# Scores of the first two pairs of heads from 64-row halves instead of stacked copies, in a fused attention and two-mixer kernel

## The chip, the cores and the metric

One core of one Trainium2 chip runs the whole program in one launch. The metric is the device time of that launch in microseconds, lower is better. Engines are named as in the profile: PE is TensorE (PEld its weight loads), DVE is VectorE, ACT is ScalarE, POOL is GpSimd, SP is the queue that issues most DMAs.

## The reference

The inputs q, k, v have 4 batches, 12 heads, 448 positions and 64 numbers a head. Everything is float32 outside; two mixers follow the attention.

```python
def _attn_ref(q, k, v, g_q, g_k):
    q_n, k_n = rmsnorm(q, g_q), rmsnorm(k, g_k)      # x / sqrt(mean(x*x) + 1e-6) * g
    scores = q_n @ k_n.T / sqrt(64)
    attn = exp(scores - max(scores))
    return (attn / (attn.sum(-1) + 1e-9)) @ v

def _moe_ref(x, U, V, w_ch1, w_ch2):
    u = x + ((x.T @ U) @ V).T
    return u + relu(u @ w_ch1) @ w_ch2               # w_ch1: 768 x 3072

def _moe2_ref(x, w_tok1, w_tok2, w_ch1, w_ch2):
    u = x + (relu(x.T @ w_tok1) @ w_tok2).T
    return u + relu(u @ w_ch1) @ w_ch2               # w_ch1: 768 x 1536
```

## The kernel before, in words

A matmul runs on a rounded float32 type, so each operand that must be exact is split into a high half (a rounded copy, on ACT) and a low half (the rest, on DVE or POOL), and a product is the sum of high by high, low by high and high by low.

Attention works on pairs of heads: 24 pairs, 48 heads. The generator `attention` (line 513) steps t from -8 over all heads. In a step t it issues the scores and probabilities of the head two ahead (`softmax`, line 450), interleaved with the weighting of the values by head t (`weigh`, line 471). Then it prepares later pairs: `turn_pair` and `split_v` for the pair of head t+3, `fetch_heads` (loads of q and k) for t+7, `load_pair` for t+5. The first 24 heads run alone; the others run beside the first mixer, advanced by the loop `run` at a fixed ratio.

`load_pair` (line 369) squares q and k (line 378; on DVE for pairs 0, 2 and 3, on POOL for the others), sums the squares on DVE (line 379), forms the reciprocal root with ACT's Ln and Exp and a Newton step (lines 381 to 389), and multiplies q and k by it (line 397), which gives qn and kn. The square tile `sq` has one buffer.

`turn_pair` (line 412) transposes qn and kn of both heads on PE into `tt` (line 418), so that rows 0 to 63 hold the first head and rows 64 to 127 the second. ACT writes the high half and DVE the low half into a tile `both` (lines 425 and 426 for q, 429 and 430 for k). `both` has one buffer for q and one for k. Since the scores need each head on all 128 rows, SP copies the halves by DMA into stacked tiles: `qs` holds a head's q, high on rows 0 to 63 and low below; `ks` holds k's high (first half) and low (second half), each twice (lines 440 to 446). Pair 0 takes 12 such copies (its ks in four pieces), each later pair 8.

`softmax` (line 450) then needs two products per chunk of 112 positions. The score tile `sc` comes from a PSUM pool of three banks. DVE takes the negated maximum (line 459), ACT the exponential with its sum (line 461), POOL and DVE the reciprocal and the scaling of two chunks at a time (lines 464 to 468).

`weigh` transposes the probabilities into `pt` (line 487), copies them (ACT and DVE) and multiplies them by the values into `pv`. `split_v` (line 403) splits the values of every second head (ACT line 149, POOL line 150).

The framework orders the instructions of each engine before the run, with its own model of time, by the order of the program and the dependences; `tc.issue_after(ins)`, used by the helper `behind(name)` (line 83), adds an edge: what the block issues on that instruction's engine stands behind it. `marks` holds the instructions by name. Each engine and the SP queue then run in that fixed order.

Of the kernel before, what the change touches and what calls it, by code (L numbers as in the profile page):

```python
# [24 lines left out]
def attention_then_two_mixers(  # L25
# [343 lines left out]
    def load_pair(b, hp, turn, qk):  # L369
# [5 lines left out]
        for i, t in enumerate((qr, kr)):  # L375
            sq = pools["at"].tile([CP, 2 * NC4, D], F32, tag="sq", bufs=AT["sq"], name="sq")
            tt = t.rearrange("p h c d -> p (h c) d")
            mul(sq, tt, tt)
            nc.vector.reduce_sum(ms[:, i], sq, axis=AX.X)
# [15 lines left out]
        for i, (nm, t, n) in enumerate((("qn", qr, qn), ("kn", kr, kn))):  # L395
            n.append(pools["at"].tile([CP, NC4, 2, D], F32, tag=nm, bufs=AT["qn"], name=nm))
            mul(
                n[0].rearrange("p c h d -> p h c d"), t, scale(i, [CP, 2, NC4, D]))
        qn, kn = qn[0], kn[0]
# [12 lines left out]
    def turn_pair(qn, kn, first=False, second=False):  # L412

        parts = []
        for n, scale in ((qn, gg), (kn, None)):
# [12 lines left out]
            else:  # L428
                nc.scalar.activation(hi, tt, AF.Copy)
                nc.vector.tensor_sub(lo, tt, f(hi))  # L430
# [3 lines left out]
        for j in range(2):  # L434
            rows = slice(j * D, (j + 1) * D)
            qs = pools["at"].tile([P, S], F32R, tag="qs", bufs=3, name="qs")
            ks = pools["at"].tile([P, 2, S], F32R, tag="ks", bufs=3, name="ks")
            for u in range(2):
                half = slice(u * D, (u + 1) * D)
                if not first:  # L440
                    nc.sync.dma_start(f(ks[half]), f(kk[rows]))
                nc.sync.dma_start(f(qs[half]), f(qq[rows, u]))
            if first:
                for i in range(2):
                    for u in range(2):
                        nc.sync.dma_start(f(ks[u * D:(u + 1) * D, i]), f(kk[rows, i]))
            res.append((qs, ks[:, 0], ks[:, 1]))
        return res

    def softmax(pr, qs, ks, kt):  # L450
        for c in range(NC4):
            if c % 2 == 0:
                sm = pools["at"].tile([CP, 2], F32, tag="sm", bufs=6, name="sm")
            sc = psum("s", [CP, S], "sc")
            cs = slice(c * CP, (c + 1) * CP)
            mm(sc, qs[:, cs], ks, True, False)
            mm(sc, qs[:, cs], kt, False, True)
            nm = pools["at"].tile([CP, 1], F32, tag="nm", bufs=8, name="nm")
            nc.vector.tensor_reduce(nm, sc, axis=AX.X, op=ALU.max, negate=True)  # L459
            p = pools["pp"].tile([CP, S], F32, tag="p", bufs=AT["p"], name="p")  # L460
            nc.scalar.activation(p, sc, AF.Exp, bias=nm, accum_out=sm[:, c % 2:c % 2 + 1])  # L461
            pr.append(p)
            if c % 2:
                nc.gpsimd.tensor_scalar_add(sm, sm, 1e-9)
                nc.vector.reciprocal(sm, sm)  # L465
                for i in range(2):
                    x = pr[c - 1 + i]
                    nc.gpsimd.tensor_scalar(x, x, sm[:, i:i + 1], 1.0, op0=ALU.mult, op1=ALU.mult)  # L468
# [44 lines left out]
    def attention(pairs, seam):  # L513
# [7 lines left out]
        def soft(h):  # L521
            if not 0 <= h < n:
                return iter(())
            probs[h] = []
            return softmax(probs[h], *turned[h // 2][h % 2])

        for t in range(-8, n):
# [4 lines left out]
            steps = [soft(t + ahead) if t >= seam or t + ahead < seam else iter(())]  # L532
# [17 lines left out]
            if 0 < h < n:  # L550
                turned[h // 2] = turn_pair(*loaded[h // 2][:2], second=h == 2)
                values[h // 2] = split_v(loaded[h // 2][2], pairs[h // 2][2])
# [4 lines left out]
            if 0 <= h < n:  # L557
                loaded[h // 2] = load_pair(
                    *pairs[h // 2][:2], h // 2, fetched.pop(h // 2))
                if h == 0:  # L560
                    turned[0] = turn_pair(*loaded[0][:2], first=True)
                    values[0] = split_v(loaded[0][2], pairs[0][2])
# [626 lines left out]
```

## Time and profile before

| | |
|---|---|
| median of 3 runs | 1529.53 us (1521.19 to 1531.46) |
| the profiled execution's own time | 1526.91 us |
| its span, first to last instruction | 1525.1 us |
| PE busy | 1436.3 us (94%) |
| DVE, POOL, ACT busy | 1170.3, 902.3, 745.6 us |
| mean granted clock of PE | 0.985 |

The durations come from the one profiled execution. A busy share is a mean over stages with different limits. In a timeline row the columns are the start in us from the span's start, the time that the merged group took, the engine (SPq is SP's queue of DMA issues), the line, the operation, out<-in, sizes, how many instructions are merged, and in brackets the idle time of the engine before, with what ended it. A matmul's row begins with its start and ends when its result is written, so two that follow closely overlap.

### The profile page before, as it was taken

What the parts mean: (1) busy time and instruction counts of PE and PEld (TensorE: products, weight loads), DVE (VectorE), ACT (ScalarE), POOL (GpSimd) and SP (SyncE); (2) the same over time, 40 slices, a digit from 0 to 9 for tenths busy, and PEclk for the clock granted to TensorE, in tenths of its full rate; (3) what the DMA queues carried; (4) which work ended last, traced back from release to release, by engine and by line L of the source; (5) the groups of instructions that cost most, each with busy time, mean ns of one, the idle gap of its engine ahead of it and who ended that gap; (6) DMA issues with size and microseconds to landing.
All of it is one profiled execution on the core that took longest, in us unless ns stands there. A gap on an engine that the chain in (4) does not pass through costs nothing.

```text
span 1525.1 us, 22086 instructions
## 1 busy us (share of the span) xinstructions
PE 1436.3 (94%) x7396; PEld 1271.5 (83%) x7396; DVE 1170.3 (77%) x1805; ACT 745.6 (49%) x1508; POOL 902.3 (59%) x943
## 2 busy tenths in 40 slices
PE   4899988999999999999999999999999999989997
PEld 3666767888888889888898998888999998979996
DVE  6888877888787788676758675477898988577886
ACT  4687755666566665444535343335343431334421
POOL 5889936777766565455655454047777755213842
PEclk9999979999999999999999999999999999999999
DMA  6676646777766565765637664355445463323343
GB/s 170 151 174 153 151 163 208 245 212 224 236 209 199 166 209 188 247 231 189 221 120 248 227 238 143 102 194 154 157 148 163 147 196 118 120 83 120 126 123 103
DMA packets 144385, 266.06 MB, mean 174 GB/s; under 512 B 12832, under 2 KB 104448, under 8 KB 144160
## 3 DMA queue, kind: packets, MB, share of 16 engines
q1 hardware_dynamic: 143952, 264.65, 55.6%
q8 instruction: 59, 0.97, 0.3%
q14 instruction: 54, 0.44, 0.1%
q10 hardware_dynamic: 320, 0.00, 0.0%
HBM read 149.72 MB, written 79.10 MB: 150 GB/s over the span
## 4 chain that ended last, share of the span: by engine, by line
PE 52%; DVE 8%; DMA 4%; POOL 3%; ACT 2%; issue 2%; SPq 0%; DVEq 0%; POOLq 0%; ACTq 0%
PE ps_x L79 23%; PE ps_p L79 10%; PE ps_g L79 10%; PE ps_t L79 2%; PE ps_u L79 2%; DVE w_bits L136 1%; DVE w_bits L131 1%; DVE w_bits L132 1%; POOL w L150 1%; PE pv L79 1%; ACT w_bits L130 1%; PE pt L487 1%; PE sc L79 1%; POOL w_bits L139 1%; DMA qs<-both 1%
## 5 line engine op out<-in xcount | busy, mean ns | idle before, releaser
L79 PE MATMUL ps_x<-gs,w 128*128 128x448 f32 x1440 | 326.0, 373 | 7.6 <-DVE gs L656 3.9
L79 PE MATMUL ps_g<-u,w 128*128 128x448 f32 x1440 | 312.7, 370 | 4.0 <-DMA w<-h_a 1.6
L79 PEld LDWEIGHTS ps_x<-gs,w 128*128 128x128 f32 x1440 | 267.9, 191 | 34.5 <-DVE gs L656 6.9
L79 PEld LDWEIGHTS ps_g<-u,w 128*128 128x128 f32 x1440 | 270.2, 189 | 27.6 <-DMA w<-h_a 1.8
L79 PE MATMUL ps_x<-gs,w_b 128*128 128x448 f32 x1026 | 226.5, 366 | 6.9 <-DVE xT L852 3.9
L139 POOL TENSOR_TENSOR w_bits<-w_bits,w_round 128x768 uint32<-128x768 uint32 (+3 forms) x80 | 145.1, 1814 | 121.0 <-DVE w_bits L136 68.9
L79 PEld LDWEIGHTS ps_x<-gs,w_b 128*128 128x128 f32 x1026 | 191.9, 188 | 24.4 <-DVE xT L852 5.0
L150 POOL TENSOR_TENSOR w<-w_bits,w 128x768 fp32r<-128x768 f32 (+3 forms) x82 | 148.1, 1816 | 82.9 <-ACT w L149 74.8
L686 DVE TENSOR_TENSOR xT<-ps_x,xT 128x448 f32<-128x448 f32 x216 | 132.2, 618 | 43.5 <-PE ps_x L79 41.2
L150 POOL TENSOR_TENSOR w_b<-w_f,w_b 128x384 fp32r<-128x384 f32 x104 | 119.0, 1157 | 68.2 <-ACT w_b L149 67.9
L468 POOL TENSOR_SCALAR p<-p,sm 112x448 f32<-112x448 f32 x192 | 131.4, 697 | 19.4 <-DVE sm L465 16.1
L79 PE MATMUL sc<-ks,qs 128*112 128x448 f32 x384 | 125.2, 412 | 18.5 <-ACT p L461 15.2
L461 ACT ACTIVATE p<-sc,nm 112x448 f32<-112x448 f32 x192 | 121.5, 635 | 37.8 <-DVE nm L459 36.4
L300 POOL TENSOR_TENSOR w_f<-w_f 128x384 f32<-128x384 f32 x26 | 29.1, 1118 | 176.1 <-DMA w_f<-c_a 99.0
L459 DVE TENSOR_REDUCE nm<-sc 112x1 f32<-112x448 f32 x192 | 116.0, 614 | 12.4 <-PE sc L79 11.9
L487 PEld LDWEIGHTS pt<-ident,p 112*112 112x112 f32 x768 | 88.6, 134 | 32.2 <-issue 9.1
L487 PE MATMUL pt<-ident,p 112*112 112x112 f32 x768 | 109.3, 260 | 3.0 <-DVE pl L502 1.9
L498 ACT ACTIVATE ph<-pt 112x448 fp32r<-112x448 f32 (+1 forms) x168 | 88.3, 545 | 38.4 <-PE pt L487 37.5
L131 DVE TENSOR_SCALAR w_bits<-w_bits 128x768 f32<-128x768 f32 (+3 forms) x80 | 65.2, 815 | 52.4 <-ACT w_bits L130 52.3
L135 ACT ACTIVATE w_round<-w_raw 128x768 uint32<-128x768 uint32 (+3 forms) x80 | 69.9, 874 | 66.4 <-POOL w_bits L139 60.0
L502 DVE TENSOR_TENSOR pl<-pt,ph 112x448 fp32r<-112x448 f32 x144 | 86.9, 615 | 18.3 <-ACT ph L498 17.8
L130 ACT ACTIVATE w_bits<-w_raw 128x768 f32<-128x768 f32 (+3 forms) x80 | 70.0, 875 | 57.5 <-POOL w L150 31.1
(141 smaller groups left out, 2718.0 us busy)
## 6 DMA issues: line engine op xcount, KB each, us to landing
w_raw<-in_moe_w_ch_dram SPq DMA_DIRECT2D x72, 768.0 KB, 5.1
w_b<-h_a SPq DMA_DIRECT2D x65, 384.0 KB, 4.3
h_a<-w SPq DMA_DIRECT2D x56, 384.0 KB, 2.7
ks<-both SPq DMA_DIRECT2D x92, 224.0 KB, 3.7
c_a<-w_bits SPq DMA_DIRECT2D x40, 384.0 KB, 4.4
w_f<-c_a SPq DMA_DIRECT2D x40, 384.0 KB, 3.1
h_b<-w SPq DMA_DIRECT2D x32, 384.0 KB, 2.5
w_b<-h_b SPq DMA_DIRECT2D x29, 384.0 KB, 3.8
```

Source lines behind the costliest of these rows:

```text
L79: nc.tensor.matmul(o, lhsT=l, rhs=r, start=start, stop=stop)
L130: nc.scalar.activation(f(w), f(high), AF.Abs)
L131: nc.vector.tensor_scalar_max(f(w), f(w), TINY)
L139: nc.gpsimd.tensor_tensor(w, w, r, op=ALU.add)
L150: nc.gpsimd.tensor_sub(lo, w, f(hi))
L459: nc.vector.tensor_reduce(nm, sc, axis=AX.X, op=ALU.max, negate=True)
L461: nc.scalar.activation(p, sc, AF.Exp, bias=nm, accum_out=sm[:, c % 2:c % 2 + 1])
L468: nc.gpsimd.tensor_scalar(x, x, sm[:, i:i + 1], 1.0, op0=ALU.mult, op1=ALU.mult)
L487: nc.tensor.transpose(pt[:, c * CP:(c + 1) * CP], pr[c][:, kc * CP:(kc + 1) * CP], ident[:CP, :CP],)
L498: nc.scalar.activation(ph, pt, AF.Copy)
L502: nc.vector.tensor_sub(pl, pt, f(ph))
L686: nc.vector.tensor_add(xT[:, dc], px, xT[:, dc])
```

## The change

For the first two pairs (heads 0 to 3) `turn_pair` is called with `direct=True`: it returns the halves in `both` themselves, on the 64 rows of each head, with three products per chunk (high by high, low by high, high by low), and makes no stacked copies. `softmax` takes several heads, each with its list of products, and issues product i of all heads before product i+1. In step t = -2 it is called for heads 0 and 1 together, so their chunks alternate and their products lie on rows 0 to 63 and 64 to 127; heads 2 and 3 follow one at a time in steps 0 and 1.

New edges: the sums of squares of pair 1 stand behind pair 0's kn on DVE; the squares of pair 2 stand behind the low half of pair 0's k; the value splits of pairs 0 and 1 are issued together in step -2, ACT's part behind the high half of pair 0's k, POOL's part behind pair 1's kn. All other pairs go as before.

```diff
-            mul(sq, tt, tt)
-            nc.vector.reduce_sum(ms[:, i], sq, axis=AX.X)
+            with behind("klo" if turn == 2 else None):
+                mul(sq, tt, tt)
+            with behind("kn" if turn == 1 else None):
+                nc.vector.reduce_sum(ms[:, i], sq, axis=AX.X)
...
-            mul(
+            ins = mul(
                 n[0].rearrange("p c h d -> p h c d"), t, scale(i, [CP, 2, NC4, D]))
+        if turn < 2:
+            marks["kn"] = ins
...
-    def turn_pair(qn, kn, first=False, second=False):
+    def turn_pair(qn, kn, first=False, second=False, direct=False):
...
-                nc.scalar.activation(hi, tt, AF.Copy)
-                nc.vector.tensor_sub(lo, tt, f(hi))
+                khi = nc.scalar.activation(hi, tt, AF.Copy)
+                klo = nc.vector.tensor_sub(lo, tt, f(hi))
+                if first:
+                    marks.update(khi=khi, klo=klo)
...
             rows = slice(j * D, (j + 1) * D)
+            if direct:
+                (qh, ql), (kh, kl) = [[x[rows, i] for i in range(2)] for x in (qq, kk)]
+                res.append([(qh, kh), (ql, kh), (qh, kl)])
+                continue
...
-                if not first:
-                    nc.sync.dma_start(f(ks[half]), f(kk[rows]))
+                nc.sync.dma_start(f(ks[half]), f(kk[rows]))
                 nc.sync.dma_start(f(qs[half]), f(qq[rows, u]))
-            if first:
-                for i in range(2):
-                    for u in range(2):
-                        nc.sync.dma_start(f(ks[u * D:(u + 1) * D, i]), f(kk[rows, i]))
-            res.append((qs, ks[:, 0], ks[:, 1]))
+            res.append([(qs, ks[:, 0]), (qs, ks[:, 1])])
...
-    def softmax(pr, qs, ks, kt):
+    def softmax(*heads):
+        sums = [None] * len(heads)
         for c in range(NC4):
...
+            scs = [psum("s", [CP, S], "sc") for _ in heads]
+            n = len(heads[0][1])
+            for i in range(n):
+                for sc, (_, products) in zip(scs, heads):
+                    l, r = products[i]
+                    mm(sc, l[:, cs], r, i == 0, i == n - 1)
...
+            hs = (0, 1) if t == -2 else (t + ahead,) if t >= 0 else ()
+            steps = [soft(*hs) if t >= seam or t + ahead < seam else iter(())]
...
-                turned[h // 2] = turn_pair(*loaded[h // 2][:2], second=h == 2)
-                values[h // 2] = split_v(loaded[h // 2][2], pairs[h // 2][2])
+                turned[h // 2] = turn_pair(*loaded[h // 2][:2], second=h == 2, direct=h == 2)
+                for i in (0, 1) if h == 2 else (h // 2,):
+                    with behind("khi" if h == 2 else None), behind("kn" if h == 2 else None):
+                        values[i] = split_v(loaded[i][2], pairs[i][2])
...
-                    turned[0] = turn_pair(*loaded[0][:2], first=True)
-                    values[0] = split_v(loaded[0][2], pairs[0][2])
+                    turned[0] = turn_pair(*loaded[0][:2], first=True, direct=True)
```

## Rows read from the trace of the kernel before

**Rows 1.** The page: TensorE's busy time, and its granted clock in 40 slices.

```profile
PE 1436.3 (94%) x7396; PEld 1271.5 (83%) x7396; DVE 1170.3 (77%) x1805; ACT 745.6 (49%) x1508; POOL 902.3 (59%) x943
PEclk9999979999999999999999999999999999999999
```

**Rows 2.** Stretches: length, busy PE, PEld, DVE, ACT, POOL (instructions), clock, DMA share, GB/s.

```profile
25.00:42.20 17.20, 13.68 (x61) 8.96 (x60) 12.79 (x28) 11.24 (x33) 13.08 (x26) 0.90 0.78 188
42.20:190.00 147.80, 135.83 (x782) 100.67 (x781) 128.64 (x264) 112.00 (x303) 131.94 (x244) 0.99 0.64 156
...
432.00:1525.10 1093.10, 1057.39 (x5381) 964.83 (x5379) 819.25 (x1146) 465.56 (x845) 581.61 (x463) 0.99 0.52 169
```

**Rows 3.** Timeline, 8 to 18 us: pair 0 up to its first scores.

```profile
8.52 0.68 DVE L379 TENSOR_REDUCE ms<-sq 112x8 f32<-112x512 f32 x1
...
9.12 0.17 DVE L389 TENSOR_TENSOR rs<-rs,nt 112x16 f32<-112x16 f32 x1
...
9.40 1.19 POOL L150 TENSOR_TENSOR vs<-vr,vs 112x256 fp32r<-112x256 f32 x1 [1.75 <-ACT vs L149]
9.92 1.22 DVE L397 TENSOR_TENSOR kn<-kr,rs 112x512 f32<-112x512 f32 x1
...
12.24 0.54 ACT L429 ACTIVATE both<-tt 128x448 fp32r<-128x448 f32 x1 [0.44 <-PE tt L418]
...
13.40 0.68 DVE L426 SCALAR_TENSOR_TENSOR both<-tt,gg,both 128x448 fp32r<-128x448 f32 x1
...
14.00 0.68 DVE L379 TENSOR_REDUCE ms<-sq 112x8 f32<-112x512 f32 x1
...
14.59 0.61 DVE L430 TENSOR_TENSOR both<-tt,both 128x448 fp32r<-128x448 f32 x1
14.66 2.47 SPq L446 DMA_DIRECT2D ks<-both  x4
...
17.72 1.43 PE L79 MATMUL sc<-ks,qs 128*112 128x448 f32 x3
```

**Rows 4.** Timeline, 22 to 34 us: pair 1, heads 1 and 2.

```profile
22.66 0.54 ACT L429 ACTIVATE both<-tt 128x448 fp32r<-128x448 f32 x1
...
25.05 2.84 SPq L441 DMA_DIRECT2D ks<-both  x4
...
27.15 0.65 PE L79 MATMUL sc<-ks,qs 128*112 128x448 f32 x2
...
29.33 1.04 PE L79 MATMUL sc<-ks,qs 128*112 128x448 f32 x4 [1.53 <-DMA ks<-both]
...
31.85 0.63 ACT L425 ACTIVATE both<-tt,gg 128x448 fp32r<-128x448 f32 x1 [2.39 <-PE pt L487]
...
33.15 1.71 PE L79 MATMUL sc<-ks,qs 128*112 128x448 f32 x4 [1.99 <-ACT p L461]
```

**Rows 5.** Timeline, 36 to 43 us: pair 2, weighting, and head 4's first scores.

```profile
36.87 2.76 SPq L441 DMA_DIRECT2D ks<-both  x4
...
40.43 0.55 PE L487 MATMUL pt<-ident,p 112*112 112x112 f32 x4
...
40.75 0.64 PE L79 MATMUL sc<-ks,qs 128*112 128x448 f32 x2
...
41.22 0.92 PE L79 MATMUL pv<-ph,vr 112*128 112x448 f32 x2
...
42.18 0.57 PE L79 MATMUL sc<-ks,qs 128*112 128x448 f32 x2
```

**Rows 6.** Tiles both and sc, first 45 us: ns min/median/max, and the copies' landing.

```profile
DMA to landing us min/median/max: 2.1/2.3/4.4
...
L459 DVE TENSOR_REDUCE nm<-sc x17: 601/615/626, 21.4 to 45.0; 112x1 f32<-112x448 f32 x17
L461 ACT ACTIVATE p<-sc,nm x16: 624/630/650, 22.0 to 44.0; 112x448 f32<-112x448 f32 x16
```

**Rows 7.** Chain of waits at 845 us: one run of products in a full stream.

```profile
845.48 14.59 PE ps_g L79 x72
```

More of the change, by code (lines that the diff above doesn't have):

```diff
@@ L448, in turn_pair @@
-        return res
-    def softmax(pr, qs, ks, kt):
+            res.append([(qs, ks[:, 0]), (qs, ks[:, 1])])
+        return res
+    def softmax(*heads):
+        sums = [None] * len(heads)
         for c in range(NC4):
-            if c % 2 == 0:
-                sm = pools["at"].tile([CP, 2], F32, tag="sm", bufs=6, name="sm")
-            sc = psum("s", [CP, S], "sc")
             cs = slice(c * CP, (c + 1) * CP)
[L456 to L468, printed above, removed]
+            scs = [psum("s", [CP, S], "sc") for _ in heads]
[4 more added lines that the diff above has]
+                    mm(sc, l[:, cs], r, i == 0, i == n - 1)
+            for h, (sc, (pr, _)) in enumerate(zip(scs, heads)):
+                if c % 2 == 0:
+                    sums[h] = pools["at"].tile([CP, 2], F32, tag="sm", bufs=6, name="sm")
+                sm = sums[h]
+                nm = pools["at"].tile([CP, 1], F32, tag="nm", bufs=8, name="nm")
+                nc.vector.tensor_reduce(nm, sc, axis=AX.X, op=ALU.max, negate=True)
+                p = pools["pp"].tile([CP, S], F32, tag="p", bufs=AT["p"], name="p")
+                nc.scalar.activation(p, sc, AF.Exp, bias=nm, accum_out=sm[:, c % 2:c % 2 + 1])
+                pr.append(p)
+                if c % 2:
+                    nc.gpsimd.tensor_scalar_add(sm, sm, 1e-9)
+                    nc.vector.reciprocal(sm, sm)
+                    for i in range(2):
+                        x = pr[c - 1 + i]
+                        nc.gpsimd.tensor_scalar(x, x, sm[:, i:i + 1], 1.0, op0=ALU.mult,
+                                                op1=ALU.mult)
@@ L519, in attention, with soft @@
         dst = None
[L521 to L525, printed above, removed]
+        def soft(*hs):
+            hs = [h for h in hs if 0 <= h < n]
+            for h in hs:
+                probs[h] = []
+            return softmax(*[(probs[h], turned[h // 2][h % 2]) for h in hs]) if hs else iter(())
         for t in range(-8, n):
@@ L531, in attention @@
                     pass
-            steps = [soft(t + ahead) if t >= seam or t + ahead < seam else iter(())]
+            hs = (0, 1) if t == -2 else (t + ahead,) if t >= 0 else ()
+            steps = [soft(*hs) if t >= seam or t + ahead < seam else iter(())]
             if t >= 0:
```

## The prediction, made before the result was known

> **What bounds the kernel now.** I read the page first. TensorE is busy for 1436.3 of 1525.1 us, and the granted clock is full in nearly every slice [rows 1]. The change touches only four of 48 heads, so the next view is the table of stretches. From 432 us to the end TensorE is busy for 1057 of 1093 us. From 42.2 to 190 us, the even run of attention, it is busy for 135.8 of 147.8 us, with GpSimd (131.9) and VectorE (128.6) close behind. Between 25 and 42.2 us it is busy for 13.68 of 17.2 us at a granted clock of 0.90 [rows 2]. So nothing after 42 us has slack worth speaking of, and the change can only shorten the ramp before it. The recorded chain of waits reaches back only to 432 us, so I argue the ramp from the timeline. If attention's even run begins x us earlier, I let the end come x us earlier, since its successors are bound by TensorE and their weight loads stand in program order behind attention.
>
> Three points of the timeline carry the argument:
> - The first score product starts at 17.72 us [rows 3].
> - The first score product of head 2 starts at 29.33 us [rows 4].
> - The first score product of head 4 starts at 42.18 us, after which the run is even [rows 5].
>
> **Part 1: the way to the first scores.** Four things in the old chain go.
> - The square sum of pair 1 at 8.52 us sits on VectorE ahead of pair 0's last Newton step and its norms. It is 0.68 long. The edge behind "kn" moves it after them, and the chain moves up by about 0.5: line 389 can start 0.1 after the place where the sum now begins, 8.6 instead of 9.12.
> - The norm of k takes 1.22 us beside GpSimd's 1.19 us subtraction for v, where VectorE's sum over as many numbers needs 0.68. That subtraction now waits until after pair 1's norms on GpSimd: 0.5 saved.
> - k's high half then starts at 12.24 - 1.0 = 11.2 and ends at 11.75. On VectorE the square of pair 2 (before 13.40) and the sum at 14.00 go behind k's low half. The low half of q can follow its high half at about 11.3, and k's low half ends near 12.65 instead of 15.2.
> - The twelve copies (the first four of one tile's ks: 14.66, taking 2.47 to issue) vanish, 2.1 us of landing included [rows 3, 6].
>
> The first complete score chunk can start at about 12.75, so **5.0 us earlier** than 17.72. What is moved is hidden: the split of v serves the weighting of head 1, which needs head 1's probabilities first, and the squares and sums serve the norms of pair 2, whose halves wait for much later scores (Part 5); VectorE is busy for only three quarters of the ramp [rows 2]. A price on the other side: GpSimd's second square of pair 1 needs the single square buffer, whose first sum now waits for "kn" and ends at about 10.8. Before, GpSimd was held by the subtraction until 9.40 + 1.19 = 10.6, so pair 1's norms come 0.2 to 0.3 later. They are covered by pair 1's wait for the buffer in Part 3; without that cover 0.3 is the cost.
>
> **Part 2: scores of heads 0 and 1.** Before, they ran from 17.72 to 27.8, ten us for eight tiles [rows 3, 4]. Now each chunk holds two tiles at once in three banks, so the second tile of a chunk waits for an exponential of the chunk before. One round is the products, a maximum (0.62) and an exponential (0.63) [rows 6], with some 0.3 of hand-over (an estimate). Six products of this width at the lower clock are 5 x 0.4 + 0.5 = 2.5 us if they run one after another (four take 1.71 us [rows 4], so 3 x 0.4 + 0.5), and half of that if the two heads' rows run side by side. No row shows a product on 64 rows; these are the two ends. I take the middle, 1.9, which gives rounds of some 3 us less the overlap of the first tile: chunks end at about 13.8, 16.6, 19.3 and 22. The ends are 20.5 and 24.
>
> **Part 3: pair 1's halves.** The tile "both" of each of q and k has one buffer. Before, pair 1's halves waited for the copies of pair 0: k's high half came at 22.66, four ks copies from 25.05, scores from 29.33 [rows 4]. Now they wait for the last score of pair 0, at 22. ScalarE's two copies are 0.63 + 0.54, VectorE's low halves some 1.3 with two maxima between them: 24.7. Without the eight copies of pair 1 the scores of head 2 start at once, **4.6 us earlier** (2.6 to 6). Behind ScalarE's waiting copy stand exponentials of pair 0, but those depend on the same scores.
>
> **Part 4: heads 2 and 3.** Three products per chunk in place of two are eight more. At 0.2 us each (72 in 14.59 [rows 7]) that is **1.6 us**; if the slow clock lasts, 3.2; if TensorE has holes there, nothing. The old stretch contains an idle ScalarE before 31.85 and the drop of the clock to its lower level, 1.2 GHz: at 33.15, after two microseconds without products, four products take 1.71 where they took 1.04 at 29.33; denser work may remove this, worth up to half of the 3.4 us that the 0.90 stands for (17.2 x 0.1 / 0.5), so 1.7 [rows 2, 4].
>
> **Part 5: pair 2, still copied.** Its high halves now wait for the last score of head 3, where before they waited only for copies into stacked tiles. From the release to head 4's first score: two ScalarE copies (1.2), k's low half (0.6 and 0.3 of hand-over), four copies at 0.59 or more to issue (36.87: 2.76 for four), 2.1 to 2.3 of landing: about 6.8 us [rows 5, 6]. Before, head 4 began 1 us after head 3's last pair of products (40.75). The cover is the weighting of heads 2 and 3, whose probabilities are there: four groups of transposes at 0.55 and two of products at 0.92 are 4.0 us a head [rows 5], two heads 8 us. I cost the wait at nothing. Bare, it is up to 5.8.
>
> **The sum**: 4.6 - 1.6 = 3.0 us off. The profiled execution took 1526.9 us (span 1525.1 plus 1.8 around it), so 1523.9 for one like it. The median of three is 2.6 above that execution, so I forecast 1529.5 - 3.0 = **1526.5 us**. Its own range is 1523 to 1529.
>
> **A rule weighed against the trace.** TensorE goes from transposes (112 rows) to scores (128 rows) and back without a hole: the two score products at 40.75 take 0.64 and the products of the weighting start 0.47 later [rows 5]. The Trainium skill (TensorEngine Tiling (Array Packing), Key Properties) says that changing the tiling mode drains TensorE, and that different tiles can run in parallel. The first speaks against three products per chunk amid full-height work, the second for Part 2's shorter end. No row shows either, and the forecast takes neither in full.
>
> **The rivals.**
> - *A. Each change between full-height work and 64-row products empties TensorE.* A drain is what one product lasts beyond its spacing, 0.64 - 2 x 0.2 = 0.24 us [rows 5, 7]. Heads 2 and 3 are interleaved with weighting, so two changes for each of eight chunks, and four more for pair 0: 20 x 0.24 = 4.8. Then 3.0 - 4.8 = 1.8 slower, 1531.3. It decides from 13 changes on. For it: TensorE is near its limit once the ramp ends. Against: the ramp still has holes of over 3 us that may take it. This is the result by the page's drain rule above. Chance 0.15.
> - *B. Part 5's wait is bare.* Place: between head 3's last score and head 4's first. ScalarE and SP run in order, so a half of pair 2 that waits for TensorE holds back the copies of the weighting that should cover it, as the copy at 31.85 held exponentials for 2.4 us. Then 5.8 is lost, less the 3.0: 2.8 slower, and a hole like that at 31 to 33 brings the low clock again, 1 to 2 us: 1533.5. It decides when under half of the 5.8 is covered. For it: one buffer, and an idle ScalarE there already. Against: two heads of ready work. Chance 0.15.
> - *C. All of the first gain arrives and the clock stays up:* 5.0 + 1.7, the eight products in holes: 6.7 off, 1522.8; with one or two later holes of attention closed by the new order it could reach 1515. Chance 0.2.
> - *D. The ramp is swallowed:* the even run is as much bound by GpSimd and VectorE as by TensorE [rows 2], and the second half of attention is paced by the loop over the first mixer. Within 1 us of before, 1529.5. Chance 0.15.
>
> **How the numbers follow.** The forecast has 0.35. The cases lie between 1515 and 1534; all runs of before lie between 1521 and 1531, so I give 1516 to 1535. A measurement of this kernel can tell about 1% (15 us) from no change. No case reaches that by its own sum; only a changed order over all of attention, which no row prices, could. Faster by over 1%: 0.06, out of C; slower: 0.03, out of A and B; within: 0.91.
>
> **What would show it.** First score product near 12.8 us, head 2's near 24.7, head 4's near 40 to 42, with transposes of heads 2 and 3 ahead of it. If pairs of 64-row products overlap, starts of heads 0 and 1 come in twos. If A holds, the gap between the last score product and the next transpose is above 0.2 us. If B holds, TensorE is idle for 3 us or more between 33 and 42 us, with a granted clock of 0.5 behind it. The prediction is wrong if head 4's first score is early and the end is not, or if the stretch after 190 us changes its length by more than the ramp does.

## The result, and the profile after

The changed kernel takes 1549.38 us (median of 6 runs, 1542.88 to 1553.11) where the kernel before took 1529.54 us beside it: a ratio of 1.0143, 95% interval 1.0112 to 1.0173. It is slower by 1.4%; 1526.5 us within 1516 to 1535 was forecast. The profiled execution has a span of 1551.3 us, 26.2 us more than that of before.

First the page after (it answers to [rows 1]), TensorE's busy time and its granted clock in 40 slices.

```profile
PE 1458.7 (94%) x7412; PEld 1279.1 (82%) x7412; DVE 1177.6 (76%) x1805; ACT 746.1 (48%) x1508; POOL 906.1 (58%) x943
...
PEclk9999988999999999999999999999999999999999
```

TensorE has 16 products more (three in place of two for 16 chunks) and is busy 22.4 us longer; no other engine gained more than 7.3 us. Next two stretches of after, columns as in [rows 2].

```profile
25.00:42.20 17.20, 14.79 (x45) 8.72 (x45) 10.29 (x21) 7.87 (x23) 14.03 (x28) 1.00 0.13 42
42.20:190.00 147.80, 134.23 (x745) 97.89 (x744) 123.23 (x255) 110.24 (x299) 122.56 (x226) 0.97 0.63 156
```

In the first, TensorE ran 45 matmuls where it ran 61, VectorE and ScalarE did less than before (10.29 and 7.87 us for 12.79 and 11.24), and the DMA share fell from 0.78 to 0.13: the work behind the ramp is held up. Now the timeline of after, 9 to 28 us, which answers to [rows 3] and the first rows of [rows 4].

```profile
9.75 0.69 DVE L399 TENSOR_TENSOR kn<-kr,rs 112x512 f32<-112x512 f32 x1
...
11.74 0.54 ACT L433 ACTIVATE both<-tt 128x448 fp32r<-128x448 f32 x1
...
12.34 2.58 PE L79 MATMUL sc<-both 64*112 64x448 f32 x9 [0.63 <-ACT both L433]
12.86 0.67 DVE L381 TENSOR_REDUCE ms<-sq 112x8 f32<-112x512 f32 x1
13.57 0.69 DVE L379 TENSOR_TENSOR sq<-qr 112x512 f32<-112x512 f32 x1
...
14.29 0.69 DVE L381 TENSOR_REDUCE ms<-sq 112x8 f32<-112x512 f32 x1
...
15.02 0.69 DVE L379 TENSOR_TENSOR sq<-kr 112x512 f32<-112x512 f32 x1
...
15.62 1.15 DVE L471 TENSOR_REDUCE nm<-sc 112x1 f32<-112x448 f32 x2
...
17.57 1.01 PE L422 MATMUL tt<-ident,qn 112*128 112x112 f32 x4 [2.65 <-POOL qn L399]
...
24.27 1.46 PE L79 MATMUL sc<-both 64*112 64x448 f32 x3
...
26.66 0.62 ACT L429 ACTIVATE both<-tt,gg 128x448 fp32r<-128x448 f32 x1
...
27.77 1.83 PE L79 MATMUL sc<-both 64*112 64x448 f32 x4 [2.04 <-ACT both L433]
```

The first scores start at 12.34 us, 5.4 us earlier. But VectorE, in order, does a sum of pair 1 and the squares and a sum of pair 2 between 12.86 and 15.62, ahead of the first maximum. TensorE's next scores stand behind pair 1's transposes, which wait for GpSimd's qn until 17.57. Pair 0's last products begin at 24.27 and end at 25.7, pair 1's q half is copied at 26.66, and head 2's scores start at 27.77: 1.6 us ahead of before's 29.33.

The same timeline from 40 to 57 us answers to [rows 5]:

```profile
40.85 2.08 PE L79 MATMUL sc<-both 64*112 64x448 f32 x9
...
45.77 0.87 PE L79 MATMUL sc<-both 64*112 64x448 f32 x3
...
46.67 0.64 ACT L429 ACTIVATE both<-tt,gg 128x448 fp32r<-128x448 f32 x1 [0.19 <-PE sc L79]
...
47.33 2.46 SPq L451 DMA_DIRECT2D qs<-both  x4
...
48.82 0.55 PE L422 MATMUL tt<-ident,kn 112*128 112x112 f32 x4
...
49.41 0.54 ACT L433 ACTIVATE both<-tt 128x448 fp32r<-128x448 f32 x1 [0.39 <-PE tt L422]
...
50.99 3.04 SPq L450 DMA_DIRECT2D ks<-both  x4
...
55.29 1.45 PE L79 MATMUL sc<-ks,qs 128*112 128x448 f32 x6 [0.40 <-issue]
```

Head 3's last products begin at 45.77; only then can pair 2's halves enter the one buffer (46.67). k's transposes stand behind weighting on TensorE (48.82), k's copies issue from 50.99, and head 4 starts at 55.29, where before had 42.18.

**Where the time comes from.** All kernels here can be compared at the same work. The table gives, from each profile, in us, the start of the first score product, of head 4's first maximum (the 17th of all), of the first product of the first mixer (ps_g), of its 658th product into ps_x (the end of the stretch in which attention runs beside the mixer), and what follows it to the end.

| profile | first score | head 4 | mixer | 658th | rest |
|---|---|---|---|---|---|
| before, [rows 1 to 7] | 17.7 | 45.0 | 208.0 | 661.6 | 863.5 |
| before, 2nd and 3rd profile | 18.1, 17.5 | 43.4, 43.0 | 205.2, 206.2 | 656.5, 662.3 | 868.7, 867.8 |
| changed | 12.3 | 56.1 | 217.2 | 676.4 | 874.9 |
| changed, 2nd profile | 11.8 | 56.6 | 220.2 | 681.2 | 870.2 |

Against the means of before (43.8, 206.5, 660.1, 866.7) the two profiles of the changed kernel are 12.6 us late at head 4, 12.2 at the mixer and 18.7 at the 658th product. The rest is 5.9 us longer, though every engine's instructions stand there in the same order as before. Ahead of it the order differs on every engine. Between the first two profiles alone, 14.8 of the 26.2 us lie before the 658th product and 11.4 in the rest; the three profiles of before differ by 5.2 us there among themselves.

### The profile page after: what moved, and what is told of

Same layout as the page of the kernel before. It is cut to its first block, busy times and chain, and to the rows that moved or that the text cites. A ratio compares the mean times of both kernels' runs of the same rounds, so it can differ in the third digit from the quotient of the medians.

```text
span 1551.3 us, 22064 instructions
## 1 busy us (share of the span) xinstructions
PE 1458.7 (94%) x7412; PEld 1279.1 (82%) x7412; DVE 1177.6 (76%) x1805; ACT 746.1 (48%) x1508; POOL 906.1 (58%) x943
## 4 chain that ended last, share of the span: by engine, by line
PE 58%; DVE 13%; POOL 8%; DMA 8%; ACT 5%; issue 5%; SPq 2%; ACTq 0%; DVEq 0%; POOLq 0%
PE ps_x L79 24%; PE ps_g L79 11%; PE ps_p L79 10%; DMA qs<-both 3%; PE pv L79 3%; PE sc L79 3%; POOL w L150 2%; POOL w_bits L139 2%; DVE w_bits L131 2%; PE pt L500 2%; PE ps_t L79 2%; PE ps_u L79 2%; DVE w_bits L136 2%; DVE w_bits L132 1%; ACT w_bits L130 1%
## 5 line engine op out<-in xcount | busy, mean ns | idle before, releaser
L79 PE MATMUL ps_x<-gs,w_b 128*128 128x448 f32 x1026 | 232.0, 371 | 7.3 <-DVE xT L867 3.9
L480 POOL TENSOR_SCALAR p<-p,sm 112x448 f32<-112x448 f32 x192 | 136.5, 724 | 25.7 <-DVE sm L477 22.1
L79 PE MATMUL sc<-ks,qs 128*112 128x448 f32 x352 | 114.6, 413 | 23.2 <-ACT p L473 22.0
L131 DVE TENSOR_SCALAR w_bits<-w_bits 128x768 f32<-128x768 f32 (+3 forms) x80 | 70.0, 875 | 55.8 <-ACT w_bits L130 55.7
L511 ACT ACTIVATE ph<-pt 112x448 fp32r<-112x448 f32 (+1 forms) x168 | 88.9, 544 | 23.3 <-PE pt L500 22.4
L806 ACT ACTIVATE pu<-pu 128x448 f32<-128x448 f32 x56 | 32.3, 578 | 133.8 <-DVE pu L795 133.4
```

The costliest lines, as they stand in the source:

```text
L79: nc.tensor.matmul(o, lhsT=l, rhs=r, start=start, stop=stop)
L131: nc.vector.tensor_scalar_max(f(w), f(w), TINY)
L511: nc.scalar.activation(ph, pt, AF.Copy)
```

## The experiments

In this part, "head n at" gives the start of that head's first maximum, "early" and "late" are against the first profile of before, and the ratio is against the kernel before, run beside it. Two theories were set against each other. **R**: the ramp loses the time, since pairs 1 and 2 wait for the last score that reads the one buffer. **O**: the framework orders every engine anew after any edit, and the new order of attention loses the time, whatever the ramp does.

### Parts of the change alone

Only the edges, put into the kernel before (pairs 0 and 1 copied as before; the split of pair 0's values moved with pair 1's), e1:

```diff
-            mul(sq, tt, tt)
-            nc.vector.reduce_sum(ms[:, i], sq, axis=AX.X)
+            with behind("klo" if turn == 2 else None):
+                mul(sq, tt, tt)
+            with behind("kn" if turn == 1 else None):
+                nc.vector.reduce_sum(ms[:, i], sq, axis=AX.X)
...
-                values[h // 2] = split_v(loaded[h // 2][2], pairs[h // 2][2])
+                for i in (0, 1) if h == 2 else (h // 2,):
+                    with behind("khi" if h == 2 else None), behind("kn" if h == 2 else None):
+                        values[i] = split_v(loaded[i][2], pairs[i][2])
```

> The kernel before with the new order edges and the later value splits alone: stacked copies and two products per chunk stay. Theory R (the loss comes from the split halves: later pairs wait for scores where they waited for copies): no loss, 1529 less up to 2 us, and the first scores about 1 to 2 us earlier than 17.7. Theory O (the framework plans a new order for all of attention, and a worse one for the stretch from 190 to 600 us, whatever the change is): the time leaves 1529.5 by 5 us or more in either direction although the ramp is hardly touched.

Measured 1534.78 us, 1.0052 (1.0026 to 1.0079): O's case, barely (5.3 us from 1529.5). Head 4's first maximum 41.7, the mixer 207.5, the 658th product 660.6. At head 12 it was 8.7 us early, and by the mixer 0.5 of it was left. At the 658th product its profile is level with the mean of before (660.1); what it loses stands in the rest (873.0).

Pair 0 alone direct (`direct=h == 2` taken out of the call for pair 1), e2:

> The changed kernel with only heads 0 and 1 direct; pair 1 is copied again. Theory R: pair 2 no longer waits for head 3's scores, so most of the 8.7 us lost by the end of the first attention stage goes: that stage ends at about 190 to 194 us instead of 199, and the time is near 1533 to 1540. Theory O: the stage after 190 us still loses some 12 us against the kernel before, time 1540 to 1550.

1549.52 us, 1.0125 (1.0096 to 1.0154); head 4 at 49.0, mixer 219.3, 658th 677.0.

Pair 1 alone direct (`direct=True` taken out of pair 0's call; heads 0 and 1 still issue their products by turns), e3:

> The changed kernel with only heads 2 and 3 direct; pair 0 is copied again. Theory R: the wait of pair 2's halves for head 3's last score stays, head 4's first score comes at 50 us or later, the time stays at 1543 or above. Theory O: nothing is tied to this wait, the time may lie anywhere between 1525 and 1550.

1558.83 us, 1.0185 (1.0150 to 1.0220); head 4 at 55.8, mixer 228.4, 658th 692.3: the worst of all, with a ramp no worse than the changed kernel's. R had 1543 or above, O 1525 to 1550, so this run is outside what O allowed; but R gives no reason for its 9 us above the changed kernel. The changed kernel once more, e4:

> The changed kernel once more, unedited, for a second profile. If the slower spacing of products from 1075 to 1260 us (206.6 ns against 202.6 in the kernel before) and the 2 to 3 us lost around 1050 us belong to its order of instructions, they come again; if they are chance of one execution, the second profile shows 202.6 ns there. The time should be 1549 within 4 us.

1551.25 us, 1.0135 (1.0110 to 1.0160). Its positions are in the first table; its late products are not spaced as in the first profile (203.2 ns for 206.7, see the last part), so that spacing is not the order's.

Every part alone was slower, and by sums that no ramp explains: e2 was 0.1 us early at head 12 (101.13 against 101.25) and 11.3 us late at the mixer. That spoke for O, as did e2's time (1540 to 1550 was O's), but each run still mixed the two.

### The suspected waits taken away

Pair 1's halves in buffers of their own, e5 (two buffers for all pairs were not tried):

```diff
-            both = pools["at"].tile([P, 2, S], F32R, tag="qq" if scale else "kk",
-                                    bufs=1, name="both")
+            own = "1" if direct and not first else ""
+            both = pools["pp" if own else "at"].tile(
+                [P, 2, S], F32R, tag=("qq" if scale else "kk") + own, bufs=1, name="both")
```

> The changed kernel, but pair 1's halves have buffers of their own, so neither pair 1 nor pair 2 waits for the last score that reads the halves before it. The order planned for all of attention changes with it. R (the loss begins where later pairs wait for scores that read the one buffer): qhi of pair 1 no longer waits for the last score of heads 0 and 1, head 4's first maximum comes back from 56 us to 45 us or before, the lower clock ends earlier than 40 us, and the first mixer product comes within 3 us of before's 208.0; the whole run loses 8 us or more of the 20 that the change costs: 1530 to 1541. O (the new order over all of attention loses the time, wherever the ramp ends): head 4 is early as well, but the first mixer product stays at 215 us or later and the whole at 1543 or more.

1544.86 us, 1.0128 (1.0097 to 1.0159). Head 4 came back to 46.5, 1.5 us short of the 45 that R set, and at head 12 the kernel was about level with before (101.9 against 101.25). But the mixer came at 219.6, the 658th product at 677.7. That is O's line: most of the wait can go and the loss stays.

Pair 0's values in a tile of their own, so that SP does not wait with a later load of values (`fetch_heads` takes one more argument), e6:

> The changed kernel, but pair 0's values have a tile of their own, so the load of pair 3's values does not wait on SP until head 0's weighting has read pair 0's. The instructions of TensorE keep their order. If the loads held up behind that wait on SP (13.3 us at 31 to 45 us) cost time: the wait is gone, the late loads of k near 57 to 79 us come some 10 us earlier, the first mixer product comes 3 to 6 us earlier than in the changed kernel, and the whole is 1543 to 1547. If they were covered: the same milestones as the changed kernel within 1 us up to 208 us, and 1549 to 1552.

1548.78 us, 1.0148 (1.0116 to 1.0180). The load of values no longer waits from 31 to 45 us, but the next load, of q, goes at 50.56 as it did at 50.46, and the mixer comes at 216.4, 0.9 before the changed kernel's, where 3 to 6 would have shown a cost. The wait was covered.

Heads 0 and 1 one after the other, e7:

```diff
-            hs = (0, 1) if t == -2 else (t + ahead,) if t >= 0 else ()
-            steps = [soft(*hs) if t >= seam or t + ahead < seam else iter(())]
+            steps = [soft(t + ahead) if t >= seam or t + ahead < seam else iter(())]
```

> The changed kernel, but heads 0 and 1 follow one another, each with its three products per chunk; nothing runs side by side on the two halves of the rows. If running side by side is worth what the starts 3 to 12 ns apart suggest, the 24 products of heads 0 and 1 take up to 12 x 0.37 = 4.5 us more at the lower clock, less what the maxima hide, and pair 1's halves come up to 3 us later. But head 0 alone is ready sooner, so its weighting can start sooner. R: head 4's first score comes no earlier than in the changed kernel (55.3 us), the whole 1549 to 1554. O: the milestones after 100 us move by several us either way, not by the ramp's difference.

1550.59 us, 1.0162 (1.0132 to 1.0193); head 4 at 54.2, the mixer at 220.7. R had head 4 no earlier than in the changed kernel; its first score came 1.7 us earlier (53.57). In the whole, side by side or not makes no difference that can be told; the order is new here too.

The edges, with the first weight's work on ScalarE behind attention's last copy, e8:

```diff
-        w1s = [w1_chunk("a", wa1, j) for j in range(G)]
+        with behind("tmp"):
+            w1s = [w1_chunk("a", wa1, j) for j in range(G)]
```

> The edges alone (as in the run with only the edges; all pairs copied), and one edge more: the first weight's work on ScalarE stands behind the copy of the last head's weighted values (tmp). If the hole of 4.7 us on TensorE before the first mixer comes from ScalarE waiting, in order, for that weight's load ahead of the last copy of attention, the hole falls under 2 us, and of the 8 us that the edges gain by 160 us at least 5 are left at the first mixer product: it comes at 201 to 204 us. The whole is then 1523 to 1530, against 1534.8 for the edges alone. If the hole has another cause it stays at 4 us or more and the whole at 1533 to 1537.

1536.27 us, 1.0070 (1.0046 to 1.0094); the mixer at 208.2. The waits of TensorE at 180 to 210 us in e1 have one line for the hole (what waited, for what, us in total, times, longest):

```profile
PE ps_h L79 <- ACT xs L583: 5.3, 2, 4.7
```

The same view of e8:

```profile
PE ps_h L79 <- ACT xs L583: 3.2, 1, 3.2
...
PE pt L493 <- POOL p L474: 1.0, 2, 0.8
```

The hole was in part ScalarE's wait, and shrank by 2.1 us, to neither of the two values expected, but the mixer did not come earlier than e1's 207.5: other waits took its place (GpSimd's 1.0 is one). The reading was too narrow.

### The order held

To part the two, the order itself was made the variable. The order of every engine of one kernel, from head 4's first score to the 658th product into ps_x, was written into another as a chain of edges; everything before head 4's first score is left to the framework. The edit, the same in all that follow (ORDER holds the numbers of some 5600 instructions, one list for each of four engines and the SP queue; `...` stands for arguments left out here):

```diff
+    def pin():
+        traced = {i.name: i for i in nc.cur_bb.bb.instructions}
+        for steps in ORDER:
+            at, before = 0, None
+            for step in steps.split():
+                at += int(step)
+                ins = traced[f"I-{at}"]
+                if before is not None:
+                    tc.add_manual_dep(ins, before.name, ...)
+                before = ins
```

The changed kernel in the order of before, e9:

> The changed kernel, with the order of the kernel before held by edges on all five engines, from head 4's first score through the mixed stage (the rest has the same order in both anyway). Heads 0 to 3, pair 1 and pair 2 stay as changed. O (the new order of all of attention costs more than the ramp): head 4's first maximum is still about 11 us late or somewhat more, since its order no longer lets the weighting go ahead of the waiting scores; but nothing more is lost after 125 us, the mixed stage takes 453 to 455 us again, and the whole comes at 1533 to 1542. R (the loss is what the ramp itself costs, and the orders are equal): 1547 to 1553.

The edges alone in the order of before, e10:

> The edges alone (as in the run with only the edges), with the order of the kernel before held on all five engines from head 4's first score through the mixed stage. O: the ramp's gain of some 3 us at head 4 is kept to the first mixer product (203 to 206 us) and to the end: 1521 to 1526, quicker than both kernels. R or the hole at the seam as a cause of its own: it loses its gain as the edges alone do, 1531 to 1536.

The kernel before in the order of the changed one, e11:

> The reverse: the kernel before, nothing of the change in it, with the order of the changed kernel held on all five engines from head 4's first score through the mixed stage. O: the ramp stays as before (head 4 at 45 us) or loses a little, the loss begins after it: 4 us or more by the first mixer product, 5 more in the mixed stage, the whole at 1535 to 1545. R: the order alone costs nothing; within 3 us of before, 1524 to 1531.

The changed kernel with pair 1's own buffers (e5) in the order of before, e12:

> The changed kernel with pair 1's halves in buffers of their own and the order of the kernel before held on all five engines from head 4's first score through the mixed stage: both suspected costs taken away. Both theories together: head 4's first maximum at 42 to 46.5 us, the first mixer product at 205 to 210 us, the whole at 1522 to 1529, so what is left of the change is worth between nothing and 5 us. If a third cause is left (the mode changes, the products added), it stays above 1531.

| kernel | its own new order | order of before held |
|---|---|---|
| changed | 1.0143 (1.0112 to 1.0173) | e9: 1543.54 us, 1.0130 (1.0099 to 1.0162) |
| changed, own buffers | e5: 1.0128 (1.0097 to 1.0159) | e12: 1531.08 us, 1.0041 (1.0018 to 1.0065) |
| edges alone | e1: 1.0052 (1.0026 to 1.0079) | e10: 1523.33 us, 0.9987 (0.9965 to 1.0010) |

From head 4 to the 658th product, by the profiles, e9, e10 and e12 run in before's order, e11 in the changed kernel's, on all four engines and the queue. The chain of edges itself costs nothing that e10 would show.

And e11, the kernel before with nothing but the changed order: 1545.39 us, **1.0146** (1.0120 to 1.0171), as much as the whole change costs. The positions in the profiles:

| profile | head 4 | head 16 (65th maximum) | mixer | 658th | rest |
|---|---|---|---|---|---|
| before, three | 45.0, 43.4, 43.0 | 128.9, 127.0, 127.3 | 208.0, 205.2, 206.2 | 661.6, 656.5, 662.3 | 863.5, 868.7, 867.8 |
| changed | 56.1 | 133.8 | 217.2 | 676.4 | 874.9 |
| e9 | 53.8 | 139.2 | 218.4 | 670.8 | 875.0 |
| e10 | 43.0 | 125.7 | 205.6 | 655.9 | 865.4 |
| e11 | 53.4 | 129.6 | 213.8 | 676.8 | 869.9 |
| e12 | 46.1 | 129.7 | 208.8 | 666.8 | 872.3 |

In e9 the ramp's loss stands unchanged to the end of the mixed stage (against the first profile of before: 10.4 us at head 16, 10.4 at the mixer, 9.2 at the 658th product): with the order held, what the ramp loses stays lost, and up to the 658th product nothing is added to it. In e11 the scores of heads 0 to 3 come as in before, and so do head 4's, but head 4's first maximum comes 8.4 us late, where O expected little:

```profile
40.47 0.63 PE L79 MATMUL sc<-ks,qs 128*112 128x448 f32 x2
...
53.37 1.67 DVE L459 TENSOR_REDUCE nm<-sc 112x1 f32<-112x448 f32 x3
```

VectorE, in the changed order, does weighting, norms and halves first and reads the first three chunks of head 4 together, as in the changed kernel, whose scores come at 55.29. All but 0.8 us of it comes back by head 16, and then 5.8 us are lost at the mixer and 15.2 at the 658th product. The stretch from the first mixer product to its 83rd product into ps_x shows it. Before (columns as in [rows 2]):

```profile
208.00:303.80 95.80, 84.49 (x429) 72.11 (x427) 78.38 (x134) 59.14 (x119) 60.27 (x61) 0.95 0.68 218
```

The changed kernel in before's order, e9:

```profile
218.40:314.50 96.10, 84.49 (x428) 71.20 (x427) 78.77 (x133) 59.19 (x119) 60.34 (x61) 0.96 0.67 216
```

The kernel before in the changed order, e11:

```profile
213.80:320.00 106.20, 91.43 (x441) 78.67 (x440) 88.53 (x140) 62.39 (x125) 67.84 (x68) 0.87 0.62 198
```

With the order of before, the changed kernel takes 96.1 us for it as before did (95.8). With the changed order, the kernel before takes 106.2: 12 matmuls more stand there, with 6.9 us more of TensorE's time and 3.5 us more without a product, at a granted clock of 0.87 (0.95 in before). The waits of TensorE in that stretch of e11:

```profile
PE sc L79 <- ACT p L461: 4.4, 2, 3.8
PE ps_g L79 <- DVE gs L656: 3.6, 1, 3.6
PE ps_u L79 <- DVE xs L605: 3.0, 3, 1.2
PE ps_g L79 <- ACT u L582: 2.0, 1, 2.0
```

Before waits 5.2 us for p and 2.4 for xs of L605 there, but never for gs; both profiles of the changed kernel wait 3.5 us for gs. So both theories were right. The ramp's waits cost some 10 us at the mixer in before's order (e9 against e12); the changed order costs the whole 1.4% on the kernel before (e11), 0.9% with own buffers (e5 against e12) and 0.65% on the edges alone (e1 against e10). The two do not add up: with the ramp as changed, before's order gains nothing that the times tell (1.0130 against 1.0143), though by its profile e9 is 8.0 us ahead of the changed kernel's mean at the 658th product; it has the longest rest of all. Part of the reason may be that an order fits its own ramp: e9 and e11 each run an order with scores that it was not made for, as the two rows of e11 show at head 4. How much of the loss that makes is not shown. e9 came 1.5 us above what O allowed, e11 0.4 above; e12 came at 1531.08, at the bound that was to mean a third cause.

### What is left, and whether anything is quicker

Only pair 0 direct, its halves in buffers of their own, pair 1 copied, the order of before, e13 (the buffers as in e5, but for `first`):

> Only pair 0's heads take scores from the split halves, and these lie in buffers of their own; pair 1 is copied into stacked tiles as before, the edges stay, and the order of the kernel before is held on all five engines from head 4's first score. If the 0.4% left with both costs taken away comes from heads 2 and 3 in three products among full-height work: first score at 12 us, head 4's first maximum at 40 to 43 us (before 45.0), the first mixer product at 203 to 206 us, the whole 1519 to 1526. If it comes from how the ramp meets the held order: head 4's first maximum at 45 to 47 us, the whole 1527 to 1534.

1526.32 us, 0.9982 (0.9960 to 1.0005); head 4 at 41.4, mixer 203.2, 658th 653.3: the first case by these positions, 0.3 us above it by the time. From e12 to e13 head 4 gains 4.7 us, so what was left in e12 goes with pair 1's direct scores. An estimate from the starts in the traces fits: e12 has eight products more at 0.37 us and ten changes more between full-height and 64-row work at some 0.23 (last part), 5.3 us together. The timeline of TensorE in e12 has head 2's scores at the lower clock, nine products in 3.70 us, where two per chunk would be six:

```profile
26.26 3.70 PE L79 MATMUL sc<-both 64*112 64x448 f32 x9
29.89 1.01 PE L422 MATMUL tt<-ident,kn 112*128 112x112 f32 x4
30.82 1.47 PE L79 MATMUL sc<-both 64*112 64x448 f32 x6
32.37 0.62 PE L501 MATMUL pt<-ident,p 112*112 112x112 f32 x2
32.92 1.46 PE L79 MATMUL sc<-both 64*112 64x448 f32 x3
```

The edges in their own order to head 12's first score (101 us in before), then before's, e14:

> The edges alone in the framework's own order up to head 12's first score (about 100 us), and from there the order of the kernel before, held on all five engines through the mixed stage. If the early gain is work done earlier: head 12's first maximum some 8.7 us before the kernel before's 101.25, still 6 to 9 us early at the first mixer product (199 to 202 us) and at the end: 1516 to 1521, quicker than both kernels. If it is only another order, with work left behind that is paid for later: at the first mixer product 0 to 4 us early, the whole 1522 to 1529.

1529.67 us, 1.0000 (0.9978 to 1.0022). At head 12 it is 3.6 us early, not 8.7, and 3.0 at the mixer, as in the second case, 0.7 us above it by the time. But holding the order from head 12 also changed the order ahead of it (head 12 came at 97.7, in e1 at 92.5), so e1's early state was not carried over. That e1's gain is the order in which work was taken, and not work saved, is likely but not shown.

The kernel before twice more, e15 and e16:

> The kernel before, unchanged, profiled again. If the length of the late stretch is the lot of an execution: 861.6-like positions agree with the first profile within 1.5 us up to the end of the mixed stage, and the late stretch comes out anywhere from 863 to 875 us. If the late stretch of the other kernels is longer because of how they reach it: it is 862 to 866 us again.

> As the run before it, once more: by the lot of an execution the three late stretches of the kernel before differ by several us; otherwise all three are 862 to 866 us.

1527.53 us (1.0012, 0.9990 to 1.0034) and 1531.85 in one run. The rest is 863.5, 868.7 and 867.8 us, above the 866 of the second case, so an execution's lot is in it; but the early positions differ too, by up to 5.7 us (656.54 and 662.28), where 1.5 was expected. So the 3 us by which e10 and e14 seem early in their profiles lie within the scatter of before. No version here is measurably quicker than the kernel before: e10 and e13 come nearest, and both intervals contain 1.

## Why the prediction was wrong

**The step that failed first is in the opening part**: "If attention's even run begins x us earlier, I let the end come x us earlier". It holds where the order is held (e9: 10.4 us at head 16 and at the mixer). The change does not hold it. I named "a changed order over all of attention, which no row prices" as the only way past 1%, and gave slower by over 1% a chance of 0.03. It was no remote case: each edit of the ramp gave a new order on all engines up to the 658th product (e1 to e3), and e11 prices the changed kernel's at 1.46%. And the even run began later, not earlier; that is the second step.

**The second is the cost of Part 5, put at nothing.** Rival B named the mechanism, and it is what the ramp shows: pair 2's halves wait for head 3's last score. B's price, 2.8 us slower, was too low, since the earlier parts did not deliver the 3.0 us that it subtracts: head 2 came 1.6 us early, head 4 13.1 late. From the release (46.67) to head 4's first score (55.29) lie 8.6 us, where I worked out 6.8: k's transposes stand behind weighting on TensorE and come 2.2 us after q's half. The weighting did go ahead (head 3's weighted values, read by VectorE, come at 66.33 against 67.02 of before), so the cover was there, for a while; but the scores behind it were 13 us late. B's sign, TensorE idle for 3 us or more, did not come between head 3's last score and head 4's first: weighting stood where the scores were to be. Own buffers took 9.6 us of the lateness away (e5, 46.5 against 56.1), its new order included.

Part by part:

- *Part 1*: first scores at 12.34 (11.78 in the second profile; forecast 12.75). k's norm took 0.69 as worked out, but k's high half came at 11.74, not 11.2; the first products needed only the high halves, and did not wait for k's low half as the forecast has it. That the two errors cancel is luck. Wrong was "what is moved is hidden", with VectorE's three quarters of busy time as the ground: VectorE works in order, and what stands ahead of the first maximum fills 12.86 to 15.62.
- *Part 2*: 22 forecast, 25.7 came, outside 20.5 to 24. The products were at the short end: nine in 2.58 us, six of them of heads 0 and 1 side by side, against 3.70 for nine of one head (e12). The round was sized by products and maxima; what set it were maxima behind squares and sums, and scores behind pair 1's transposes, which waited for GpSimd. So halving the products bought little: from the first product of the pair to the end of its last, 13.4 us side by side and 14.5 one after the other (e7).
- *Part 3*: head 2 gained 1.6 us, not 4.6, because Part 2 ended late. The release itself took 2.0 us from the last score, where I allowed 2.7.
- *Part 4*: 1.6 us at the full clock, 3.2 at the lower. The lower was the case, and more: 4.7 us between e12 and e13. Rival A's changes are a part of it: about 0.23 us each at the lower clock, close to the 0.24 that A worked out, and about 0.16 at the full (last part). After has 16 of them where A counted 20, so 2.6 to 3.7 us in sum, some of it in holes of the ramp. By A's own sign they would have been missed: the gap of the starts before the next transpose grows by 0.13 only, and the rest shows at the transpose behind it.
- *The gain of the clock* went the other way. In after, four products take 1.83 us at 27.77 and nine take 2.08 at 40.85; in before four took 1.04 at 29.33 [rows 4]. By the starts of its products after stays at the lower level, 1.2 GHz, until about 40 us, where before left it near 27 but for a dip at 33 to 37; the 1.00 in the clock column of the stretch from 25 us stands against these spacings (the trace has no clock record before 40.4 us). TensorE was busy for 14.79 of 17.2 us in that stretch.
- *The rule weighed*: the Trainium skill (TensorEngine Tiling (Array Packing), Key Properties) says that different tiles run in parallel and that a mode change drains TensorE. The first is seen here, in nine products in 2.58 us. Of the second the trace shows a price for each change, given below; whether that is a drain no row tells.

The prediction named as a sign of being wrong that "the stretch after 190 us changes its length by more than the ramp does". It came: in e5's profile head 4 is 1.5 us late and the end 16.1.

**What stays open.** The rest after the 658th product, with its order unchanged, takes 863.5 to 875.0 us in eighteen profiles, 863.5 to 868.7 in three of before, 870.2 and 874.9 in two of the changed kernel. So some 6 us (against the means of before) to 11 (between the first two profiles) of the 26 may be the lot of the executions; whether the late stretch inherits something was not settled. e9's whole is 1.3% slower, about 20 us, of which its profile shows 9.2 up to there and 11.5 behind it. A profile is one execution: e12's took 1540.9 us, 9.8 above the median of its runs, e9's 4.0 above, e2's 5.2 below. Why the new order loses in the mixed stage was traced to where it waits, not to the rule by which the framework chose it. Nor is it shown why the edges alone lose 0.5%, since their profile is level at the 658th product.

## What to carry to other kernels

Where a framework orders the engines from the whole program, an edit of the first 40 us is an edit of the order of everything behind it: hold the old order by edges to price the edit, and put the new order on the old kernel to price the order. A tile read directly by TensorE is held until the last score; with one buffer that wait moves to the next pair, and a busy share says nothing of what stands in line ahead of the instruction that matters.

## What the runs showed of the hardware

- Products on rows 0 to 63 and on rows 64 to 127 run side by side: in after their starts lie 3 to 12 ns apart, and nine products, of which six in such pairs, take 2.58 us where nine of one head take 3.70 (e12).
- A change between full-height and 64-row products costs some 0.2 us, and the first start alone does not show it all. From the last transpose to the third score product behind it are 1.21 us with 64-row products and 0.94 with full-height ones at the lower clock (0.69 and 0.50 at the full); from the last score product to the second transpose behind it 0.74 and 0.55 (0.43, one case in e7, and 0.30). That is 0.27 us going in and 0.19 coming out at the lower clock, 0.19 and 0.13 at the full (medians over all profiles, where no wait lies between).
- From 1073 us of before on, the products stand in the same order in all kernels. Over 411 products into ps_x there, with those into ps_p between them 825, their starts lie 202.7 to 202.9 ns apart on average in nine profiles, 206.7 in three (after, e1 and e9) and 203.2 to 205.6 in six; that is 167.2 us against 170.5 at the ends. One kernel shows several: before 202.7, 205.6 and 204.4, the changed kernel 206.7 and 203.2. So it belongs to the execution, not to the order; what chooses was not found.
